# Reading streamed weights straight from their inputs instead of from a contiguous scratch copy, with separate tail buffers, in a recurrent-memory kernel

## The chip, the cores and the metric

The kernel runs on one core of one Trainium2 chip. The metric is the device time of one execution in microseconds (us), taken as the median of several executions.

The views name the engines thus: PE is TensorE (matmuls) and PEld its weight loads, DVE is VectorE, ACT is ScalarE, POOL is GpSimd; SP is SyncE, which here only issues loads and stores (DMA transfers). HBM is the memory that holds the inputs and the scratch. The granted clock is the share of TensorE's full clock that the profile shows.

## The reference

Two layer pairs A, B, A, B over a sequence of 2048 tokens of width 640. A is attention in 64 segments of 32 tokens with 8 memory rows; segment s needs the memory that segment s-1 left, so A is a recurrence. B is a token-mixing MLP. All tensors are bf16.

```python
def _A_ref(x, mem0, Wq, Wk, Wv, Wo, seg_len):     # 32 heads of 192, M = 8 memory rows
    for s in range(n_seg):                          # 64 segments of 32 tokens, one after the other
        h = jnp.concatenate([mem, xs], axis=1)      # 40 rows
        q, k, v = ...                               # h @ Wq, Wk, Wv: each 640 x 6144
        o = softmax(mask(q k^T * scale)) v          # per head
        o = jnp.einsum('bhte,hed->btd', o, Wo)      # 6144 x 640
        mem = o[:, :M, :]; outs.append(o[:, M:, :])
def _B_ref(x, w1, w2, w3, w4):
    h = gelu(layernorm(x) @ w1)                     # 640 x 640
    ...                                             # shift a quarter of the columns by -1, +1, -2, +2 tokens
    x1 = x + shifted @ w2                           # 640 x 640
    return x1 + gelu(layernorm(x1) @ w3) @ w4       # 640 x 1536 x 640
x = x + A(LN(x)); x = x + B(LN(x)); x = x + A(LN(x)); x = x + B(LN(x))
```

## The kernel before

The kernel runs both A layers as two lanes, the second lane 6 segments behind the first, so there are 70 recurrent steps of 80 rows. In each step the attention weights are used once. They are cut into 64 half-weights of 480 KB ([128, 1920] bf16): q, k, v and output weights, 8 head groups, 2 halves. 37 of them stay resident, 27 are streamed in every step through a ring of 6 buffers. The weights of B (13 pieces w1 to w4, some 6.7 pieces per step on average) go through the same ring. Loads are issued in program order on SP's queue.

At the start the kernel copies the 27 streamed half-weights (on ACT's queue) and all of B's weights (on POOL's queue) from the inputs into scratch in HBM, laid out so that each of the 128 partitions reads one contiguous piece of 3840 B:

```python
RING_BUFS = 6
N_RES_HALVES = 37 if B2X else 26
RELAYOUT = 1
...
def w_src(kind, g, hf):
    if kind == "q":
        return Wq_v[:, :, GW * g + GWH * hf:GW * g + GWH * (hf + 1)]     # [128, 5, 384]: runs of 768 B
    ...
    return Wo_v[:, g, GCH * hf:GCH * (hf + 1), :]                        # [128, 3, 640]: runs of 1280 B
...
if RELAYOUT == 1:
    for u_ in streamed:                                                  # 27 half-weights
        nc.scalar.dma_start(out=w_view(wS[stream_idx[u_]], kind), in_=w_src(kind, g, hf))
        relaid.add(u_)
...
zt = wringB.tile([P, HSZ], bf16, name=BNAME)
nc.vector.memset(zt[:], 0.0)
for i, (nm, a, b, used) in enumerate(BP):                                # B's weights into scratch wB
    if nm == "w1":
        nc.gpsimd.dma_start(out=dst, in_=w1_v[:, :, a * P:b * P])
    ...                                                                  # w3, w4 alike
    else:                                                                # w2: zero, then the used rows
        nc.gpsimd.dma_start(out=wB[i][:, 0:used], in_=zt[:, 0:used])
        ...

def get_wB(nm, a):
    t = wringB.tile([P, HSZ], bf16, name=BNAME)                          # the shared ring
    nc.sync.dma_start(out=t[:, 0:used], in_=wB[i][:, 0:used])
    return bp_view(t, nm, a_, b_)

def get_w(kind, g, hf):
    if u_ in resident:
        return resident[u_]
    if u_ in res_set:                                                    # first use, in step 0
        nc.sync.dma_start(out=w_view(t, kind), in_=w_src(kind, g, hf))
        ...
    t = wring.tile([P, HSZ], bf16, name="wst")
    if RELAYOUT and u_ in relaid:
        nc.sync.dma_start(out=t[:], in_=wS[stream_idx[u_]])              # contiguous
    else:
        nc.sync.dma_start(out=w_view(t, kind), in_=w_src(kind, g, hf))   # original layout
```

After step 69 a tail is left: the last blocks of B. They share single buffers (`xw`, `bu`, `vT`, `bv_c`), and gelu has one scratch tile `g_sq`, so a chunk of gelu must be over before the next one begins:

```python
def gelu2(z_ps, out_ap, shape):
    sq = work.tile([P, GELU_W], f32, name="g_sq", bufs=1)
    nc.scalar.activation(out=sqv, in_=z_ps, func=ACT.Square)
    nc.vector.tensor_scalar(...); nc.vector.tensor_tensor(...)
    nc.scalar.activation(out=thv, in_=sqv, func=ACT.Tanh, scale=GELU_C)
    nc.vector.scalar_tensor_tensor(out=out_ap, ...)
...
def sA():                                          # b2x_stages: first of a block's stages
    xw = work.tile([XB, Dm], f32, name="xw", bufs=1)
    ...                                            # load rows of x1d, x3d
    u = work.tile([XB, Dm], f32, name="bu", bufs=1)
```

## Time and profile before

| | |
|---|---|
| median | 4443.05 us (4 runs), 4448.39 us (16 runs, with those beside the changed kernel) |
| step 1 begins (start) | 143.1 us |
| step 1 to step 69, start to start (middle) | 4153 us, 61.1 us a step from step 4 on |
| last attention matmul to the end (tail) | 85.4 us |

Each step opens with one matmul that clears the accumulator `psy`, so its start times cut the run into steps. This is the view of that source line between 130 and 230 us; the last columns are the first and the last start in the window:

```profile
L515 PE MATMUL psy<-zer x2: 337/337/337, 143.1 to 195.2; 128*128 128x400 bf16 x2
```

The table of stretches of the kernel before has, after each stretch, the busy us of PE, PEld (weight loads), DVE, ACT and POOL with the number of instructions, then the granted clock, the DMA share and GB/s:

```profile
0.00:50.00 50.00, 11.04 (x143) 9.11 (x143) 10.12 (x30) 0.00 (x0) 22.30 (x48) 0.90 0.99 355
50.00:100.00 50.00, 9.72 (x122) 7.89 (x123) 4.37 (x13) 8.32 (x27) 1.58 (x6) 0.56 1.05 365
100.00:150.00 50.00, 41.10 (x777) 35.22 (x774) 18.82 (x51) 18.91 (x74) 3.55 (x12) 0.97 1.06 366
200.00:4200.00 4000.00, 3579.76 (x67338) 3191.89 (x67402) 2465.50 (x6597) 1846.26 (x6917) 517.09 (x1423) 0.96 0.82 277
```

The first three rows are the start: DMA share at or above 0.99, 355 to 366 GB/s, and PE busy for only 21 of the first 100 us. (The share is the sum of packet times over 16 engines; the records of the first 100 us show up to 23 packets in flight at once, so it can pass 1.) The last row is the middle: DMA share 0.82, PE busy 3580 of 4000 us. What PE waits for there (engine, line, waited for, us in all, times, longest us):

```profile
PE pso L654 <- ACT PT L372: 155.7, 128, 10.8
PE psy L675 <- DVE oT L374: 114.5, 129, 1.7
PE pss L610 <- DVE kT L374: 100.1, 32, 7.9
...
PE y2A L1069 <- DMA wst<-wB: 1.8, 4, 0.8
...
PEld L675 <- DMA wst<-wS: 0.7, 1, 0.7
```

PE's large waits are for PT on ACT and for oT and kT on DVE, the handoffs of attention. For weights (`wst` is a buffer of the ring) it waits 1.8 us in 4000 at this line and 2.3 us in all; its weight loads (PEld) wait 0.9 us. DMA is busy for four fifths of the time, and PE is hardly ever held up by it.

In the tail, PE's last transposes for attention begin at 4358.36 us, and the two remaining blocks end with ACT's copy of `bv_c`. Timeline of the kernel before (start us, us, engine, line, what; in brackets the idle time before it and what ended it):

```profile
4358.36 0.47 PE L696 MATMUL psyt<-ident,yT 128*80 128x128 bf16 x5 [0.58 <-ACT yT L685]
...
4405.49 0.72 ACT L1083 CAST bv_c<-xw 128x640 bf16<-128x640 f32 x1 [3.63 <-DVE xw L1073]
...
4406.94 0.62 ACTq L962 DMA_DIRECT2D xw<-x3d  x1
...
4421.32 0.61 DVE L409 TENSOR_SCALAR bv_c<-bu,lnmv_b,lnrs_b 128x640 bf16<-128x640 f32 x1 [0.73 <-POOL lnrs_b L404]
...
4425.27 0.49 ACT L419 ACTIVATE g_sq<-psh 128x384 f32<-128x384 f32 x1 [1.85 <-PE psh L1056]
...
4428.05 0.49 ACT L419 ACTIVATE g_sq<-psh 128x384 f32<-128x384 f32 x1 [0.68 <-DVE h2T L423]
...
4438.98 0.72 ACT L1083 CAST bv_c<-xw 128x640 bf16<-128x640 f32 x1 [3.28 <-DVE xw L1073]
```

The first block ends with the copy at 4405.49. Only then is the second block's `xw` loaded (4406.94), and its layer norms run until 4421.3 (the last `bv_c<-bu` on DVE). The Square steps of gelu (`ACT ACTIVATE g_sq<-psh`) then follow each other at 2.8 us (4425.27, 4428.05), one chunk at a time.

### The profile page before, as it was taken

What the parts mean: (1) busy time and instruction counts of PE and PEld (TensorE: products, weight loads), DVE (VectorE), ACT (ScalarE), POOL (GpSimd) and SP (SyncE); (2) the same over time, 40 slices, a digit from 0 to 9 for tenths busy, and PEclk for the clock granted to TensorE, in tenths of its full rate; (3) what the DMA queues carried; (4) which work ended last, traced back from release to release, by engine and by line L of the source; (5) the groups of instructions that cost most, each with busy time, mean ns of one, the idle gap of its engine ahead of it and who ended that gap; (6) DMA issues with size and microseconds to landing.
All of it is one profiled execution on the core that took longest, in us unless ns stands there. A gap on an engine that the chain in (4) does not pass through costs nothing. (4 is left out here: it accounts for less than half of the span.)

```text
span 4443.2 us, 168838 instructions
## 1 busy us (share of the span) xinstructions
PE 3867.6 (87%) x72349; PEld 3440.2 (77%) x72420; DVE 2650.9 (60%) x7089; ACT 1988.7 (45%) x7427; POOL 577.5 (13%) x1578
## 2 busy tenths in 40 slices
PE   2798989898889988898988999988998988989895
PEld 2687878787778887787877888877887877888883
DVE  1455656666656666666666666666666666566654
ACT  1444444444444444444444444444444444444442
POOL 2111111111111111111111111111111111111110
PEclk7999999999999999999999999999999999999997
DMA  9887878888888788888888888888888888888884
GB/s 358 295 271 255 275 270 272 282 284 276 279 288 279 266 283 278 281 285 277 277 275 277 294 283 280 269 275 281 288 277 289 275 273 286 282 278 275 272 276 162
DMA packets 404193, 1232.59 MB, mean 277 GB/s; under 512 B 47080, under 2 KB 88176, under 8 KB 403440
## 3 DMA queue, kind: packets, MB, share of 16 engines
q1 hardware_dynamic: 378632, 1190.97, 78.9%
q10 hardware_dynamic: 21016, 23.76, 1.7%
q8 instruction: 566, 9.27, 0.8%
q0 software_dynamic: 3792, 7.05, 0.4%
q14 instruction: 187, 1.53, 0.1%
HBM read 1202.10 MB, written 38.50 MB: 279 GB/s over the span
## 5 line engine op out<-in xcount | busy, mean ns | idle before, releaser
L624 ACT ACTIVATE Pm<-pss,nb 80x80 bf16<-80x80 f32 x2240 | 699.5, 320 | 292.2 <-DVE nb L619 210.3
L568 PEld LDWEIGHTS <-hT 128*80 128x80 bf16 x5600 | 617.5, 119 | 211.4 <-issue 2.2
L372 ACT CAST V<-psv 80x384 bf16<-80x384 f32 x1120 | 507.4, 479 | 361.7 <-PE psv L568 277.5
L568 PE MATMUL psv<-wv,hT 128*80 128x384 bf16 x3500 | 663.9, 327 | 1.2 <-DMA wv<-in_A_Wv_dram 1.2
L374 DVE CAST oT<-pso 128x480 bf16<-128x480 f32 x560 | 367.5, 656 | 478.4 <-PE pso L659 476.2
L530 PEld LDWEIGHTS <-wst 128*128 128x128 bf16 x14700 | 637.2, 104 | 3.8 <-DMA wst<-wS 2.7
L374 DVE CAST kT<-psk 128x480 bf16<-128x480 f32 x560 | 364.7, 651 | 424.3 <-PE psk L530 422.6
L592 POOL COPY Vz<-V 80x128 bf16<-80x128 bf16 x560 | 169.1, 302 | 2887.0 <-ACT V L372 2874.3
L530 PE MATMUL psq<-hT,wq 128*128 128x80 bf16 x10500 | 497.4, 207 | 29.9 <-ACT hT L494 17.9
L530 PEld LDWEIGHTS <-wq 128*128 128x128 bf16 x10500 | 455.4, 103 | 38.5 <-issue 29.4
L372 ACT CAST qT<-psq 128x480 bf16<-128x480 f32 x560 | 307.6, 549 | 383.0 <-PE psq L530 381.1
L675 PE MATMUL psy<-oT,wst 128*128 128x80 bf16 x7350 | 361.0, 204 | 123.2 <-DVE oT L374 121.0
L675 PE MATMUL psy<-oT,wo 128*128 128x80 bf16 x9450 | 445.8, 204 | 1.5 <-DMA wo<-in_A_Wo_dram 1.5
L624 ACT ACTIVATION_READ_ACCUMULATOR Pm<-pss,nb 80x1 f32 x2240 | 442.1, 197 | 0.0
L675 PEld LDWEIGHTS <-wst 128*128 128x128 bf16 x7350 | 318.2, 101 | 151.9 <-issue 146.9
L568 PE MATMUL psv<-wst,hT 128*80 128x384 bf16 x2100 | 418.8, 331 | 1.2 <-DMA wst<-wS 1.1
L530 PE MATMUL psk<-hT,wst 128*128 128x80 bf16 x8400 | 411.7, 206 | 1.4 <-DMA wst<-wS 1.3
L530 PE MATMUL psk<-hT,wk 128*128 128x80 bf16 x8400 | 410.2, 206 | 2.9 <-DMA wk<-in_A_Wk_dram 2.9
L675 PEld LDWEIGHTS <-wo 128*128 128x128 bf16 x9450 | 388.4, 102 | 1.9 <-DMA wo<-in_A_Wo_dram 1.9
L372 ACT COPY PT<-pst 80x320 bf16<-80x320 bf16 x560 | 242.4, 433 | 274.0 <-PE pst L642 226.5
L610 PEld LDWEIGHTS <-qT 128*80 128x80 bf16 x3360 | 228.0, 123 | 168.1 <-issue 114.0
L374 DVE CAST kTz<-psk 64x160 bf16<-64x160 f32 x1120 | 351.9, 314 | 10.3
(122 smaller groups left out, 5896.5 us busy)
## 6 DMA issues: line engine op xcount, KB each, us to landing
wst<-wS SPq DMA_DIRECT2D x1890, 480.0 KB, 4.9
wst<-wB SPq DMA_DIRECT2D x395, 480.0 KB, 5.2
wst<-wB SPq DMA_DIRECT2D x71, 320.0 KB, 4.7
x1d<-xs SPq DMA_DIRECT2D x64, 80.0 KB, 4.0
xs<-x2d SPq DMA_DIRECT2D x64, 80.0 KB, 3.5
x3d<-xs SPq DMA_DIRECT2D x64, 80.0 KB, 3.5
xw<-x1d ACTq DMA_DIRECT2D x31, 160.0 KB, 3.9
x2d<-xw SPq DMA_DIRECT2D x31, 160.0 KB, 5.4
```

The costliest lines, as they stand in the source:

```text
L372: nc.scalar.copy(out=out_ap, in_=in_ap)
L374: nc.vector.tensor_copy(out=out_ap, in_=in_ap)
L530: nc.tensor.matmul(out=psq[:, c, :], lhsT=w[:, kc, cc * P:(cc + 1) * P], rhs=hT[:, kc, :], start=(kc == 0), stop=(kc == KC - 1))
L568: nc.tensor.matmul(out=psv[:], lhsT=hT[:, kc, :], rhs=wv[:, kc, :], start=(kc == 0), stop=(kc == KC - 1))
L592: nc.gpsimd.tensor_copy(out=vz[:, :, 0, 0:64], in_=V3[:, SS, 0:64])
L610: nc.tensor.matmul(out=o_, lhsT=l_, rhs=r_, start=False, stop=(n == len(ops) - 1))
L624: nc.scalar.activation(out=E[:, i, :], in_=pss[:, i, :], func=ACT.Exp, bias=nb[:], scale=scale, accum_out=sums[:, i:i + 1])
L675: nc.tensor.matmul(out=cx.psy[:, m, :], lhsT=wo[:, cc, m * P:(m + 1) * P], rhs=oT[:, c, :], start=False, stop=last)
```

## The change

The intent is to leave out the copies at the start and to read the weights from the inputs in every step; the price is shorter packets. Only w2 keeps its scratch copy, because its pieces are padded with zeros. In the tail, the blocks get alternate buffers, under tags whose attention tiles are no longer in use, and gelu gets three scratch tiles. Flags of other variants (`B_MERGE`, `RELAY_SPREAD`) are added but off. The core of the diff, with cuts:

```diff
-RELAYOUT = 1
+WB_LATE = 1
+B_MERGE = 0
+TAIL_ALT_TAGS = 1
+RELAY_SPREAD = 0
+RELAYOUT = 0
...
-        zt = wringB.tile([P, HSZ], bf16, name=BNAME)
-        nc.vector.memset(zt[:], 0.0)
-        for i, (nm, a, b, used) in enumerate(BP):
-            ... (all of w1, w2, w3, w4 into wB)
+        def setup_wB():
+            zt = h2T[:].rearrange("p f x -> p (f x)")
+            for i, (nm, a, b, used) in enumerate(BP):
+                if nm != "w2":
+                    continue
+                ... (zero rows, then w2's rows, on POOL's queue)
...
         def get_wB(nm, a):
             t = wringB.tile([P, HSZ], bf16, name=BNAME)
-            nc.sync.dma_start(out=t[:, 0:used], in_=wB[i][:, 0:used])
-            return bp_view(t, nm, a_, b_)
+            v = bp_view(t, nm, a_, b_)
+            if nm == "w1":
+                nc.sync.dma_start(out=v, in_=w1_v[:, :, a_ * P:b_ * P])
+            elif nm == "w3":
+                nc.sync.dma_start(out=v, in_=w3_v[:, :, a_ * P:b_ * P])
+            elif nm == "w4":
+                nc.sync.dma_start(out=v, in_=w4_v[:, a_:b_, :])
+            else:
+                nc.sync.dma_start(out=t[:, 0:used], in_=wB[i][:, 0:used])
+            return v
...
-    def gelu2(z_ps, out_ap, shape):
+    def gelu2(z_ps, out_ap, shape, tag=None):
+        if tag is None:
+            sq = work.tile([P, GELU_W], f32, name="g_sq", bufs=1)
+        else:
+            sq = work.tile([P, GELU_W], f32, name="g_sq_alt", tag=tag, bufs=(3 if PIPE_DEEP else 2))
...
+        alt = bool(TAIL_ALT_TAGS) and t >= T_A and t == T_A + (T_A % 2)
+        tg_x = "xs1" if alt else None
+        alt_g = bool(TAIL_ALT_TAGS) and t >= T_A
+        tg_v = "V" if alt_g else "vT"
...
-            xw = work.tile([XB, Dm], f32, name="xw", bufs=1)
+            xw = work.tile([XB, Dm], f32, name="xw", bufs=1) if not alt else work.tile([XB, Dm], f32, name="xw_alt", tag=tg_x)
... (bu, vT, v2T and bv_c alike; gelu2(..., tag=(tg_v if alt_g else None)))
...
+        if B2X and t >= 1 and wB_pending:
+            wB_pending.pop()()
```

More of the change, by code (lines that the diff above doesn't have):

```diff
@@ L283, with emit_relayout @@
     relaid = set()
-    if RELAYOUT == 1:
-        for u_ in streamed:
+    relay_pending = list(streamed) if RELAYOUT == 1 else []
+    def emit_relayout(n):
+        for _ in range(min(n, len(relay_pending))):
+            u_ = relay_pending.pop(0)
             kind, g, hf = u_
@@ L288 @@
             relaid.add(u_)
+    if RELAYOUT == 1 and not RELAY_SPREAD:
+        emit_relayout(len(relay_pending))
     def chunks3(n):
@@ L312, in bp_view @@
             return ap2d[:, 0:(b - a) * Dm].rearrange("p (v d) -> p v d", v=b - a)
-        zt = wringB.tile([P, HSZ], bf16, name=BNAME)
-        nc.vector.memset(zt[:], 0.0)
-        for i, (nm, a, b, used) in enumerate(BP):
-            dst = bp_view(wB[i], nm, a, b)
-            if nm == "w1":
-                nc.gpsimd.dma_start(out=dst, in_=w1_v[:, :, a * P:b * P])
-            elif nm == "w3":
-                nc.gpsimd.dma_start(out=dst, in_=w3_v[:, :, a * P:b * P])
-            elif nm == "w4":
-                nc.gpsimd.dma_start(out=dst, in_=w4_v[:, a:b, :])
-            else:
-                nc.gpsimd.dma_start(out=wB[i][:, 0:used], in_=zt[:, 0:used])
-                for v_ in range(a, b):
-                    kc, p0, p1, off = W2P[v_]
-                    nc.gpsimd.dma_start(out=dst[p0:p1, v_ - a, :], in_=B_w2[kc * P + p0:kc * P + p1, :])
+        def setup_wB():
+            zt = h2T[:].rearrange("p f x -> p (f x)")
+            for i, (nm, a, b, used) in enumerate(BP):
+                dst = bp_view(wB[i], nm, a, b)
+                if nm != "w2":
+                    continue
+                else:
+                    for z0 in range(0, used, Dm):
+                        nc.gpsimd.dma_start(out=wB[i][:, z0:z0 + Dm], in_=zt[:, 0:Dm])
+                    for v_ in range(a, b):
+                        kc, p0, p1, off = W2P[v_]
+                        nc.gpsimd.dma_start(out=dst[p0:p1, v_ - a, :], in_=B_w2[kc * P + p0:kc * P + p1, :])
+        wB_pending = [setup_wB]
+        if not WB_LATE:
+            wB_pending.pop()()
         def get_wB(nm, a):
@@ L412 @@
     GELU_W = max(6 * XS, 3 * XB) if B2X else 6 * XS
-    def gelu2(z_ps, out_ap, shape):
+    def gelu2(z_ps, out_ap, shape, tag=None):
         _, a_, b_ = shape
-        sq = work.tile([P, GELU_W], f32, name="g_sq", bufs=1)
+        if tag is None:
+            sq = work.tile([P, GELU_W], f32, name="g_sq", bufs=1)
+        else:
+            sq = work.tile([P, GELU_W], f32, name="g_sq_alt", tag=tag, bufs=(3 if PIPE_DEEP else 2))
         sqv = sq[:, 0:a_ * b_].rearrange("p (a b) -> p a b", a=a_)
@@ L946, in b2x_stages @@
         TOK = 2 * SEG
+        alt = bool(TAIL_ALT_TAGS) and t >= T_A and t == T_A + (T_A % 2)
+        tg_x = "xs1" if alt else None
+        alt_g = bool(TAIL_ALT_TAGS) and t >= T_A
+        tg_v = "V" if alt_g else "vT"
+        if alt:
+            bvt = work.tile([XB, Dm], bf16, name="bv_alt", tag="xs0")
+        else:
+            bvt = bv_c
         def sA():
-            xw = work.tile([XB, Dm], f32, name="xw", bufs=1)
+            xw = work.tile([XB, Dm], f32, name="xw", bufs=1) if not alt else work.tile([XB, Dm], f32, name="xw_alt", tag=tg_x)
             if any((not v) or kp == NP2 or kp == 0 for (_, _, _, kp, v) in items):
@@ L965, in sA @@
                     nc.gpsimd.dma_start(out=xl_c[Lb:4:2, :], in_=src[TOK * kp + TOK - 2:TOK * kp + TOK, :])
-            u = work.tile([XB, Dm], f32, name="bu", bufs=1)
+            u = work.tile([XB, Dm], f32, name="bu", bufs=1) if not alt else work.tile([XB, Dm], f32, name="bu_alt", tag=tg_x)
             st.u, st.xw, st.ranges = u, xw, ranges
@@ L972, in sA @@
             layer_norm(xw, u, slice(0, XB))
-            layer_norm(u, bv_c, slice(0, XB))
+            layer_norm(u, bvt, slice(0, XB))
             layer_norm(xl_c, xl_c, slice(0, 4))
@@ L983, in sA3 @@
         def sA3():
-            ln_apply(st.h2, bv_c)
+            ln_apply(st.h2, bvt)
             ln_apply(st.hl2, xl_c)
@@ L989, in sB @@
             for kc in range(KC):
-                nc.tensor.transpose(out=psvT[:, kc, :], in_=bv_c[:, kc * P:(kc + 1) * P], identity=ident[:, :])
+                nc.tensor.transpose(out=psvT[:, kc, :], in_=bvt[:, kc * P:(kc + 1) * P], identity=ident[:, :])
             psl = ps_tile([P, KC, XP], bf16, "psl")
@@ L993, in sB @@
                 nc.tensor.transpose(out=psl[:, kc, :], in_=xl_c[0:XP, kc * P:(kc + 1) * P], identity=ident[0:XP, 0:XP])
-            vT = work.tile([P, KC, XB + 4], bf16, name="vT", bufs=1)
+            vT = work.tile([P, KC, XB + 4], bf16, name="vT", bufs=1) if not alt else work.tile([P, KC, XB + 4], bf16, name="vT_alt", tag=tg_v, bufs=(3 if PIPE_DEEP else 2))
             evac(vT[:, :, 0:XB], psvT[:], "act")
@@ L1009, in f @@
                     nc.vector.tensor_copy(out=hTB[:, :, 0:4, :], in_=hTB[:, :, TOK:TOK + 4, :])
-                gelu2(psh[:, 0:b - a, :], hTB[:, a:b, 4:4 + TOK, :].rearrange("p k w l -> p k (w l)"), [P, b - a, XB])
+                gelu2(psh[:, 0:b - a, :], hTB[:, a:b, 4:4 + TOK, :].rearrange("p k w l -> p k (w l)"), [P, b - a, XB], tag=(tg_v if alt_g else None))
                 if last:
@@ L1035, in sD @@
             else:
-                layer_norm(u, bv_c, slice(0, XB))
+                layer_norm(u, bvt, slice(0, XB))
         def sD2():
-            ln_apply(st.h3, bv_c)
+            ln_apply(st.h3, bvt)
         def sE():
@@ L1043, in sE @@
             for kc in range(KC):
-                nc.tensor.transpose(out=psv2T[:, kc, :], in_=bv_c[:, kc * P:(kc + 1) * P], identity=ident[:, :])
-            v2T = work.tile([P, KC, XB + 4], bf16, name="v2T", tag="vT", bufs=1)
+                nc.tensor.transpose(out=psv2T[:, kc, :], in_=bvt[:, kc * P:(kc + 1) * P], identity=ident[:, :])
+            v2T = work.tile([P, KC, XB + 4], bf16, name="v2T", tag="vT", bufs=1) if not alt else work.tile([P, KC, XB + 4], bf16, name="v2T_alt", tag=tg_v, bufs=(3 if PIPE_DEEP else 2))
             evac(v2T[:, :, 0:XB], psv2T[:], "act")
@@ L1057, in f @@
                                          rhs=v2T[:, kc, 0:XB], start=(kc == 0), stop=(kc == KC - 1))
-                gelu2(psh2[:, 0:b - a, :], h2T[:, a:b, :], [P, b - a, XB])
+                gelu2(psh2[:, 0:b - a, :], h2T[:, a:b, :], [P, b - a, XB], tag=(tg_v if alt_g else None))
             return f
@@ L1082, in sG @@
                 else:
-                    nc.scalar.copy(out=bv_c[:], in_=xw[:])
-                    nc.sync.dma_start(out=dst[t0_ + j0:t0_ + j1, :], in_=bv_c[2 * j0 + Lb:2 * j1:2, :])
+                    nc.scalar.copy(out=bvt[:], in_=xw[:])
+                    nc.sync.dma_start(out=dst[t0_ + j0:t0_ + j1, :], in_=bvt[2 * j0 + Lb:2 * j1:2, :])
         has_new = any(v and kp < NP2 for (_, _, _, kp, v) in items)
@@ L1103, in b2x_stages, with mg @@
         stages.append(sG)
+        if B_MERGE and LN_SPLIT and has_new and t < T_A:
+            def mg(f1, f2):
+                return lambda: (f1(), f2())
+            i3 = stages.index(sA3)
+            stages[i3:i3 + 2] = [mg(sA3, sB)]
+            i5 = stages.index(sD2)
+            stages[i5:i5 + 2] = [mg(sD2, sE)]
+            if len(stages) > NG:
+                rest = stages[NG:]
+                spread = []
+                for f in rest:
+                    spread += [f, None]
+                stages = stages[:NG] + spread
         return stages
@@ L1112 @@
     for t in range(TT):
+        if RELAY_SPREAD and t >= 1 and relay_pending:
+            emit_relayout(RELAY_SPREAD)
+        if B2X and t >= 1 and wB_pending:
+            wB_pending.pop()()
         if B2X:
```

## The prediction

> **What bounds it now.** There are 70 recurrent steps and a tail. From 200 to 4350 us the stretch table has PE busy about 0.90, DVE 0.62, ACT 0.46, DMA 0.82. A step takes 61 us. The waits of PE there name ACT PT (158 us), DVE oT (118) and DVE kT (102); waits for DMA sum to about 3 us. So the middle is bound by PE and its handoffs, not by DMA. The ends differ. Start: step 1 begins only at 143 us; until then DMA share is 0.99 to 1.06 (about 52 MB), PE busy 11 of the first 50 us and 10 of the next 50. Tail: the last step ends near 4367 us, then two blocks of the second layer run one after the other, to 4406 and to 4443 us (chain that ended last).
>
> **What the change does.**
> 1. It drops the copies of 27 streamed half-weights and of the second layer's weights (except w2) into contiguous scratch. Step 0 still loads 64 half-weights of 480 KB once. Packet records: 768 B takes 36 ns, 1280 B 55 ns, 3840 B 149 ns clean (179 on average in the middle). 48 halves x 40 packets x 36 ns plus 16 x 24 x 55 ns per DMA engine are about 90 us, so I estimate step 1 to begin near 100 us: gain 43 us (35 to 50).
> 2. In every step the streamed loads read the original layout: five 768 B (q, k, v) or three 1280 B (output weights) packets per partition in place of one of 3840 B. Clean cost per load and engine: 1.19 us becomes 1.44 or 1.32. The Trainium skill, "DMA: Bandwidth & Descriptors", Specifications, puts line rate at 512 B and above; this trace differs: 768 B moves 21.3 B/ns, 3840 B 25.8. This adds some 470 us of 16-engine time: DMA share 0.82 to about 0.9, packets 0.40 to about 1.37 million. The order of loads and of PE's work stays beyond the first steps. Loads now land 4.9 us after issue (median), then wait 4.5 us (median; lowest 5%: 0.9) for first use. Landing 0.3 to 1 us later, few become late, mainly w4 chunks and q/k ones: loss 20 us (estimate), up to 90.
> 3. The tail gets alternate buffers: the second block's load and three layer norms (4407 to 4422 us) move under the first block, and gelu chunks (2.8 us each in series) overlap down to DVE's 1.5 us. Gain 24 us (15 to 30).
>
> **Sum.** 4443 - 43 - 24 + 20 = about 4396 us, 1.1% faster. Range (8 in 10) 4355 to 4445. Faster by over 2%: 0.08; within 2%: 0.84; slower by over 2%: 0.08.
>
> **What would show it.** Step 1 beginning at 95 to 108 us; middle DMA share near 0.9 with steps still 61 to 61.5 us; PE's waits for wst growing from 3 us to tens of us; issue to landing rising to 5.3 to 6.5 us; after the last step, 76 us shrinking to about 52.
>
> **What would make it wrong.** The large risk is the middle: the queue is near saturation, and lateness grows steeply. If the stray slow packets (179 against 149 ns) grow with the number of packets, each load costs 1.7 to 1.9 us against 1.75 us of PE time per load, and steps become DMA-bound: 100 to 300 us lost. If they come from the scratch copy, or vanish when the queue is backed up (768 B packets averaged 37 ns in the start), the loss is nil, and the result near 4375.

## More of the kernel before

Executions of one and the same kernel spread by about 1% here (4420.64 to 4464.68 us for the kernel before, 16 runs), so effects below some 10 us are read from the trace, not from the total.

## The result, and the profile after

The changed kernel takes 4392.28 us (median of 10 runs, 4381.82 to 4399.65), against 4448.39 us (16 runs). Its time over that of the kernel before is 0.9875 (95% interval 0.9856 to 0.9893). All ratios here are the mean time of one kernel's fast runs over that of the other's of the same rounds, so not quite the ratio of the medians. The outputs are correct.

In the profiled runs (4443.2 and 4384.4 us) the 58.8 us come from these parts:

| part | before | after | difference |
|---|---|---|---|
| start: to the beginning of step 1 | 143.1 us | 101.9 us | -41 |
| middle: step 1 to step 69 | 4153 us | 4158 us | +4 |
| step 69 itself | 61.5 us | 61.6 us | 0 |
| tail: last attention matmul to the end | 85.4 us | 63.4 us | -22 |

The opening matmul of steps 1 and 2 after (L537 is the old L515):

```profile
L537 PE MATMUL psy<-zer x2: 337/338/338, 101.9 to 153.9; 128*128 128x400 bf16 x2
```

The stretches of the changed kernel:

```profile
0.00:50.00 50.00, 32.08 (x373) 24.89 (x373) 17.44 (x50) 11.76 (x39) 19.07 (x51) 0.80 1.02 322
50.00:100.00 50.00, 35.63 (x528) 28.10 (x524) 13.80 (x37) 14.43 (x57) 2.93 (x10) 0.83 1.09 338
100.00:150.00 50.00, 46.99 (x934) 41.77 (x935) 25.25 (x69) 23.86 (x90) 5.92 (x19) 1.00 1.01 307
200.00:4200.00 4000.00, 3582.40 (x67454) 3194.04 (x67518) 2464.28 (x6584) 1848.59 (x6927) 512.27 (x1417) 0.96 0.92 278
```

PE now works from the first slice on (32 of the first 50 us, where it was 11). The start is still bound by DMA: share 1.02 and 1.09. In the middle the DMA share rose from 0.82 to 0.92 at the same 277 to 278 GB/s: the same bytes take more engine time. PE's busy time there is 3582 us where it was 3580. The queue lines of the two pages (queue, packets, MB, share of 16 engines), before and then after:

```profile
q1 hardware_dynamic: 378632, 1190.97, 78.9%
q10 hardware_dynamic: 21016, 23.76, 1.7%
```

```profile
q1 hardware_dynamic: 1367304, 1190.97, 89.1%
...
q10 hardware_dynamic: 5096, 10.49, 0.8%
```

1.37 million packets in place of 0.38 million move the same 1190.97 MB. PE's waits in the middle, after:

```profile
PE pso L676 <- ACT PT L391: 167.2, 124, 6.8
PE psy L697 <- DVE oT L393: 115.6, 130, 1.7
PE pss L632 <- DVE kT L393: 87.0, 31, 6.0
...
PEld L552 <- DMA wst<-in_A_Wk_dram: 2.3, 5, 0.9
...
PE psk L552 <- DMA wst<-in_A_Wk_dram: 1.5, 4, 0.8
```

PE's waits for weights are 1.5 us in 4000 (2.3 before), those of its weight loads 2.5 us (0.9 before). Next to nothing of the longer loads reached PE. The tail, after:

```profile
4321.67 0.47 PE L718 MATMUL psyt<-ident,yT 128*80 128x128 bf16 x5 [0.58 <-ACT yT L707]
...
4350.78 0.61 DVE L428 TENSOR_SCALAR bu<-xw,lnmv_b,lnrs_b 128x640 f32<-128x640 f32 x1 [0.27 <-POOL lnrs_b L423]
...
4354.29 0.61 DVE L428 TENSOR_SCALAR bv_c<-bu,lnmv_b,lnrs_b 128x640 bf16<-128x640 f32 x1 [0.26 <-POOL lnrs_b L423]
...
4363.33 0.72 ACT L1113 CAST bv_alt<-xw_alt 128x640 bf16<-128x640 f32 x1 [3.28 <-DVE xw_alt L1103]
...
4371.62 0.49 ACT L441 ACTIVATE g_sq_alt<-psh 128x384 f32<-128x384 f32 x1 [1.91 <-PE psh L1086]
4373.22 0.49 ACT L441 ACTIVATE g_sq_alt<-psh 128x384 f32<-128x384 f32 x1 [1.11 <-PE psh L1086]
...
4380.93 0.72 ACT L1113 CAST bv_c<-xw 128x640 bf16<-128x640 f32 x1 [2.67 <-DVE xw L1103]
```

The second block's layer norms (`bu<-xw` at 4350.78, `bv_c<-bu` at 4354.29) now lie before the first block's end (4363.33), and the Square steps follow each other at 1.6 us. From the transposes at 4321.67 the first block takes 42.4 us (47.9 before); from its end to the end of the program, with the second block, it is 20.3 us more (37.0 before).

### The profile page after: what moved, and what is told of

The parts are those of the page before. It is cut to its first block, busy times and chain, and to the rows that moved or that the text cites. A ratio compares the mean times of both kernels' runs of the same rounds, so it can differ in the third digit from the quotient of the medians.

```text
span 4384.4 us, 168796 instructions
## 1 busy us (share of the span) xinstructions
PE 3877.9 (88%) x72349; PEld 3446.1 (79%) x72420; DVE 2649.8 (60%) x7088; ACT 1988.7 (45%) x7427; POOL 571.7 (13%) x1573
## 3 DMA queue, kind: packets, MB, share of 16 engines
q1 hardware_dynamic: 1367304, 1190.97, 89.1%
## 5 line engine op out<-in xcount | busy, mean ns | idle before, releaser
L552 PEld LDWEIGHTS <-wk 128*128 128x128 bf16 x8400 | 351.4, 102 | 5.7 <-DMA wk<-in_A_Wk_dram 5.7
```

The costliest lines, as they stand in the source:

```text
L552: nc.tensor.matmul(out=psq[:, c, :], lhsT=w[:, kc, cc * P:(cc + 1) * P], rhs=hT[:, kc, :], start=(kc == 0), stop=(kc == KC - 1))
```

## The experiments

Theory: the total is a sum of three separate parts. The start shrinks because it is bound by DMA time and there is less of it. The middle does not move, because the loads have slack before PE needs them and a step's DMA time stays under 61 us. The tail shrinks through its buffers. Rivals: the second layer's (B's) copies alone hold the start; the tail gains from the direct loads; the layout does cost the middle, and noise hides it; the middle is free because slow packets vanish when the queue is backed up.

"Step" below is the mean step from step 4 to step 69 of the profiled run. Over all runs of the two layouts with 37 resident half-weights and 6 buffers it varies from 60.9 to 61.5 us without order, so a difference of 0.3 us in it (20 us in all) means nothing in a single profile.

### Which part of the change gives which part of the gain

**tail_only**: the kernel before, with the tail's alternate buffers alone (the changed kernel with `RELAYOUT = 1` and the old copying and loading of B's weights).

> The kernel before with the tail's alternate buffers alone. Additive theory (start -41, middle about +4, tail -22 us): 22 us less than before, ratio 0.995; step 1 still begins at 143 us, 63 us from the last attention matmul to the end in place of 85. Rival (the tail gained because the last weight loads come straight from the inputs, not from the buffers): no gain, tail stays at 80 to 85 us, ratio 0.999 to 1.000.

Measured: ratio 0.9954 (0.9927 to 0.9981), median 4434.55 us against 4454.58. Step 1 begins at 145.1 us and the tail is 66.3 us. So the buffers shorten the tail without any direct load; the rival falls.

**tail_off**: the changed kernel with

```diff
-TAIL_ALT_TAGS = 1
+TAIL_ALT_TAGS = 0
```

> The changed kernel without the tail's alternate buffers. Additive theory: 37 us less than before, ratio 0.9917; step 1 begins at 102 us, tail 85 us, steps 61.2 us. Rival (direct loading speeds the tail, not the buffers): tail near 63 us, ratio 0.987.

Measured: ratio 0.9907 (0.9881 to 0.9934), 4413.8 us. Step 1 begins at 100.8 us, the tail is 85.6 us, a step 61.27 us. The direct loads do nothing for the tail. The two halves of the change add up: 0.46% and 0.93% make 1.39%, where the whole gave 1.25% (0.0107 to 0.0144).

**a_direct**: the kernel before with

```diff
-RELAYOUT = 1
+RELAYOUT = 0
```

> The kernel before with only the attention weights loaded straight from the inputs; the second layer's weights are still copied to scratch at the start and read from there, and the tail is as before. If the start is bound by DMA time alone: 27 copies of 1.44 us less, 27 loads 0.24 us slower, so about 32 us off, step 1 at 110 to 116 us; ratio 0.993. Rival (it is the second layer's copies, which go first in the queue of POOL, that hold the start): step 1 at 130 us or later, ratio 0.997 or more. In the middle DMA share 0.90.

Measured: ratio 0.9917 (0.9891 to 0.9943), 4418.79 us. Step 1 begins at 114.9 us, a step is 60.9 us, the DMA share from 200 to 4300 us is 0.90.

**b_direct**: the changed kernel with

```diff
-TAIL_ALT_TAGS = 1
+TAIL_ALT_TAGS = 0
-RELAYOUT = 0
+RELAYOUT = 1
```

> The changed kernel with the attention weights still copied to scratch at the start, without the tail's buffers; only the second layer's weights come straight from the inputs, w2 copied late. If the start is bound by DMA time alone: some 6 MB of copies less, 15 to 18 us off, step 1 at 125 to 129 us, ratio 0.996. Rival (the second layer's copies hold the start): step 1 at 115 us or earlier, ratio 0.994 or less. In the middle DMA share 0.83.

Measured: ratio 0.9976 (0.9947 to 1.0005), 4439.06 us. Step 1 begins at 130.3 us, a step is 61.31 us, the DMA share 0.83.

The opening matmul of step 1, a_direct first, then b_direct:

```profile
L515 PE MATMUL psy<-zer x1: 337/337/337, 114.9 to 114.9; 128*128 128x400 bf16 x1
```

```profile
L537 PE MATMUL psy<-zer x1: 337/337/337, 130.3 to 130.3; 128*128 128x400 bf16 x1
```

So dropping the attention copies takes 28 us off the start and dropping B's copies 13 us; together they make the 41 us of the changed kernel. The start is a sum of DMA work, and no single queue holds it. Both estimates from DMA time (32 and 15 to 18 us) were a little too high.

### Is the middle really free, and why

**spread**: the changed kernel, with the attention copies brought back, two per step from step 1 on, so that from step 15 on the layout would be contiguous again:

```diff
-RELAY_SPREAD = 0
-RELAYOUT = 0
+RELAY_SPREAD = 2
+RELAYOUT = 1
```

> The changed kernel, but the contiguous scratch for the attention weights comes back bit by bit: two half-weights are copied to it per step from step 1 on, and each is read from it once it is copied (from step 15 on all are); step 0 reads straight from the inputs, so the start stays at 102 us. DMA share in the middle back near 0.83. My theory (the direct layout costs the middle little, 0 to 16 us): total within 15 us of the changed kernel, ratio to before 0.983 to 0.990. Rival (the middle does lose the 20 to 40 us that more DMA time could cost, hidden in the noise): 20 to 40 us faster than the changed kernel, ratio 0.979 to 0.983.

Measured: ratio 0.9932 (0.9908 to 0.9955), 4423.28 us, so neither number came true. Step 1 began at 132.8 us, not at 102. The timeline of ACT shows why:

```profile
0.81 0.73 ACTq L294 DMA_DIRECT2D wS<-in_A_Wq_dram  x1
...
47.13 0.64 ACTq L294 DMA_DIRECT2D wS<-in_A_Wq_dram  x1
...
61.23 0.56 ACTq L294 DMA_DIRECT2D wS<-in_A_Wk_dram  x1
```

The copies depend on nothing, and all 27 were issued in step 0, from 0.81 to 85.5 us; their place in the program's loop meant nothing. Which source a load reads is fixed by the program, though: loads of attention weights still come straight from the inputs until 922 us, fewer in each step. But the run still answers the question about the middle, because from step 14 on, small shifts of the order aside, it is the changed kernel with contiguous loads of the attention weights. Stretch from 300 to 4200 us, spread first, then the changed kernel:

```profile
300.00:4200.00 3900.00, 3498.93 (x65831) 3116.11 (x65829) 2407.65 (x6438) 1798.23 (x6753) 498.02 (x1385) 0.96 0.84 278
```

```profile
300.00:4200.00 3900.00, 3494.52 (x65785) 3116.12 (x65849) 2408.96 (x6438) 1804.55 (x6763) 500.20 (x1383) 0.96 0.91 278
```

DMA share 0.84 against 0.91, PE busy 3499 against 3495 us, steps 61.16 against 61.21 us, step 1 to 69 in 4155 against 4158 us. From step 15 to step 69, where all attention loads of spread are contiguous, a step takes 61.00 against 61.01 us. The direct layout costs the middle nothing that can be seen; the total of spread is 31 us above the changed kernel's, and its start 31 us longer.

**res31_after, res34_after**: the changed kernel with fewer resident half-weights, so 33 or 30 streamed per step in place of 27:

```diff
-N_RES_HALVES = 37 if B2X else 26
+N_RES_HALVES = 31 if B2X else 26      (res34_after: 34)
```

> The changed kernel with 31 resident half-weights in place of 37, so 33 streamed per step in place of 27. Theory (the middle is free only while the DMA time of a step stays under the step's 61 us; 768 B packets cost 41.6 ns in the middle, busy or not, so 1.66 us per load): 33 x 1.61 + 6.5 x 1.6 + 2 = about 65 us of DMA time per step, so the middle becomes DMA-bound: steps of 64 to 67 us, DMA share 1.0 or more, PE waits for wst over 100 us in all, total about 4640 us, ratio 1.045. Rival (slow packets vanish when the queue is backed up, 1.44 us per load): 57 us of DMA time, steps stay under 62 us, ratio under 1.00.

> The changed kernel with 34 resident half-weights, 30 streamed per step, between the 27 of the changed kernel (steps 61.2 us, DMA share 0.92) and the 33 of the run before (64.9 us, share 1.00). Theory: 30 x 1.61 + 12 = 60 us of DMA time per step against 61 us of the other work: at the edge, steps 61.8 to 63 us, share 0.97 or 0.98, PE waits for wst 20 to 80 us in all, total 4430 to 4510 us, ratio 0.995 to 1.015. If the loss grows in proportion to packets instead (half of the 3.7 us per step), steps are 63 us or more.

**res31_before**: the same edit (31) in the kernel before.

> The kernel before with the same 31 resident half-weights: same extra loads from the contiguous scratch, 1.44 us each with the slow packets. Theory: 39.5 x 1.44 + 2 = 59 us of DMA time per step, just under the 61 us: steps 61 to 62.5 us, DMA share about 0.95, start some 7 us longer (more copies), ratio 1.003 to 1.02. If the layout of the loads does not matter, it is as slow per step as the changed kernel with 31.

Measured:

| kernel | streamed per step | ratio to before | step | DMA share, 300 to 4200 us |
|---|---|---|---|---|
| changed | 27 | 0.9875 | 61.2 us | 0.91 |
| res34_after | 30 | 0.998 (0.9949 to 1.001) | 62.2 us | 0.97 |
| res31_after | 33 | 1.0433 (1.0398 to 1.0468) | 64.9 us | 1.00 |
| before | 27 | 1 | 61.1 us | 0.82 |
| res31_before | 33 | 1.0046 (1.0005 to 1.0086) | 61.6 us | 0.91 |

The stretch lines of res31_after and then res31_before:

```profile
300.00:4200.00 3900.00, 3401.45 (x61838) 2952.90 (x61895) 2278.29 (x6072) 1704.16 (x6353) 456.35 (x1293) 0.95 1.00 307
```

```profile
300.00:4200.00 3900.00, 3480.05 (x65392) 3087.29 (x65452) 2399.23 (x6399) 1784.22 (x6714) 483.80 (x1375) 0.97 0.91 324
```

And PE's largest waits for weights in the same window of res31_after:

```profile
PE y2A L1099 <- DMA wst<-in_B_w_dram: 40.6, 116, 1.8
PE psk L552 <- DMA wst<-in_A_Wk_dram: 19.0, 49, 0.8
...
PE psh L1086 <- DMA wst<-in_B_w_dram: 11.0, 32, 0.6
PE psv L590 <- DMA wst<-in_A_Wv_dram: 8.7, 21, 1.0
```

With 33 loads a step, the direct layout fills DMA's time, and the step becomes what the DMA time says: 65 us expected, 64.9 measured. (A share of 1.00 alone would not prove this, since the start showed up to 1.09; the match of step and DMA time is the stronger sign.) With 30 loads it is at the edge, as expected: share 0.97, PE's waits for wst 35 us. Read contiguously, the same extra loads cost 0.5 us a step; there the share was expected as 0.95 and came out at 0.91, for the 3840 B packets took 169.6 ns on average and not 179.5. The expected waits of res31_after (over 100 us) are met within the precision of the view: PE's waits for wst sum to 99 us, those of PEld, which may overlap with them, to 135 us. Engine time, not bytes, is what runs out: res31_before moves 324 GB/s at a share of 0.91, res31_after only 307 GB/s at 1.00. The rival falls: 768 B packets took 41.6 ns on average in the middle of the changed kernel, 41.2 ns in res31_after; they do not get back to the clean 36 ns (the median in the changed kernel) when the queue is full. (These means are over the packet records between 1000 and 4300 us.)

**ring4_after, ring4_before**: both kernels with fewer stream buffers.

```diff
-RING_BUFS = 6
+RING_BUFS = 4
```

> The changed kernel with 4 stream buffers in place of 6. Theory (the later landing of the direct loads is absorbed by the slack that 6 buffers give): a replay of the load and use times of the kernel before with 4 buffers puts 91 to 125 us of waits into the middle, steps 62.5 to 63 us, PE waits for wst near 100 us, total about 4490 us, ratio 1.01. Rival (the slack plays no part): steps still 61.2 us, ratio 0.9875.

> The kernel before with 4 stream buffers in place of 6. Theory: the replay puts 24 to 50 us of waits into the middle, steps 61.4 to 61.9 us, total about 4480 us, ratio 1.008; so with 4 buffers the direct layout costs 60 to 75 us more in the middle than the contiguous one, where with 6 it costs none that is seen. Rival: no difference between the two layouts in the middle.

Measured: ring4_after 1.0431 (1.0393 to 1.0469), 4641.13 us, steps 64.8 us, DMA share 0.88; ring4_before 1.0422 (1.038 to 1.0463), 4639.82 us, steps 64.0 us, DMA share 0.80. PE's waits for weights from 300 to 4200 us, ring4_before:

```profile
PE y2A L1069 <- DMA wst<-wB: 39.0, 66, 2.9
PE psy L675 <- DMA wst<-wS: 34.2, 48, 2.2
PE psq L530 <- DMA wst<-wS: 32.1, 37, 2.4
...
PE psk L530 <- DMA wst<-wS: 10.5, 17, 1.9
```

The totals with 4 buffers are equal, although the changed kernel starts 42 us earlier and its tail is 19 us shorter; so its middle is some 60 us longer (53 us between the starts of steps 1 and 69 in the profiles). The difference of the layouts came out near the low end of what was expected (60 to 75 us) or just under it, and this with free DMA time: it is lateness, not capacity. Pairing each load's issue, landing and first use (as at the end of this text) shows the slack: from issue to first use it is 6.1 us (before) and 6.2 us (changed) with 4 buffers, where it is 9.3 us in both kernels with 6, and between landing and first use only 1.2 and 0.8 us are left, where it was 4.5 and 3.9 us. The size of the loss itself was expected wrong: 24 to 50 us for the kernel before where nearly 190 us were lost (2.9 us a step over 65 steps), 91 to 125 us for the changed kernel where the middle grew by 244 us. The replay only knew buffers and DMA time. It kept the old order on SP's queue, where weight loads stand in line with the stores and loads of rows, and with 4 buffers the built kernel has another order there (219 of the 2716 issues on that queue stand elsewhere). Whether that is the cause was not tested.

### The parts of the tail, and the rest of the start

**tail_blocks**: the changed kernel with gelu's single scratch tile, the blocks' buffers kept:

```diff
-gelu2(psh[:, 0:b - a, :], ..., tag=(tg_v if alt_g else None))
+gelu2(psh[:, 0:b - a, :], ..., tag=None)                          (both calls)
```

> The changed kernel, with the gelu scratch of the tail single again; the two blocks keep their separate buffers. Predicted parts of the tail's gain: 16 us from the second block's load and layer norms moved under the first, 8 us from overlapped gelu chunks. So the tail should be 63 + 8 = 69 to 71 us and the total 8 us above the changed kernel, ratio 0.989. Rival (most of the gain is the gelu overlap): tail 75 us or more.

Measured: ratio 0.9878 (0.9858 to 0.9898), 4399.6 us; tail 72.2 us. So 9 us of the tail's gain come from gelu's scratch tiles and 13 us from the blocks' buffers; the total is too noisy to tell the 9 us, the trace tells it.

**w2_after0**: the changed kernel issues its copies of w2 not in step 1 but at 6.7 to 30 us, since they too depend on nothing. Here the zero rows are made from the output of step 0:

```diff
-            zt = h2T[:].rearrange("p f x -> p (f x)")
+            yf = pending_xnew[0].yT[:].rearrange("p k n -> p (k n)")
+            zt = const.tile([P, Dm], bf16, name="zw")
+            for z0 in range(0, Dm, KC * NS):
+                z1 = min(Dm, z0 + KC * NS)
+                nc.vector.tensor_scalar_mul(out=zt[:, z0:z1], in0=yf[:, 0:z1 - z0], scalar1=0.0)
```

> The changed kernel, with the zero rows for w2's scratch computed as 0 times the output of step 0, so that the 2.1 MB of w2 copies cannot start before step 0 ends (in the changed kernel they are issued from 7 us on, though the code means them for step 1). If the start is bound by DMA time: 2.1 MB at 330 GB/s are 6 us, so step 1 begins at 95 to 98 us in place of 102, and the rest stays: total 4 to 6 us below the changed kernel, ratio 0.986 to 0.987. Rival (step 0 is held by the chain of loads and matmuls, not by DMA time): step 1 still at 101 to 102 us. The first second-layer block may wait for w2 if it comes too late: then the stretch from step 1 to step 4 grows beyond 182 us.

Measured: ratio 0.9869 (0.9849 to 0.989), 4400.11 us against 4451.99. Step 1 begins at 96.5 us, as DMA time says. But step 1 then takes 60.7 us where it took 51.9, and from step 1 to step 4 it is 188.5 us (178.7 in the changed kernel), beyond the 182 us that the expectation warned of. PE's waits in step 1 of w2_after0:

```profile
PE psk L556 <- DMA wst<-in_A_Wk_dram: 2.2, 2, 2.0
...
PE psv L594 <- DMA wst<-in_A_Wv_dram: 1.4, 1, 1.4
```

The changed kernel has 0.4 us of such waits in its step 1. The copies, now in step 1, stand beside its streamed loads, and loads come late; PE's waits for wst in step 1 are 4.2 us in all, 3.8 us more than in the changed kernel, of the 8.7 us. The granted clock from 100 to 150 us was also lower (0.93 against 1.00); how much of the rest that explains was not tested. What the start saved is given back either way. The interval overlaps that of the changed kernel, and no kernel is shown to be faster than it.

## Why the prediction was right

- The total was predicted as 4396 us, 1.1% faster, and came out at 4392.28 us, ratio 0.9875. That the two are only 4 us apart is in part luck: the prediction took 47 us off a median of 4 runs (4443.05 us), and measured against the 16 runs (4448.39 us) the change is 56 us. The chance put on "within 2%" (0.84) was on the right side.
- Start: predicted -43 us with step 1 near 100 us, measured -41 us and 101.9 us. The mechanism is shown by a_direct and b_direct (28 + 13 us), and once more by w2_after0.
- Tail: predicted -24 us, measured -22 us, shown by tail_only and tail_off. The parts, which the prediction did not size, were put at 16 and 8 us before tail_blocks ran and measured as 13 and 9 us.
- Middle: the DMA share rose to 0.92 (predicted 0.9), packets to 1.376 million (1.37), landing after issue to 5.3 to 5.6 us (5.3 to 6.5), steps stayed at 61.2 us. The added engine time was somewhat less than predicted: the main queue's packets took 400 us more of 16 engines' time, not 470. The term that was mis-sized most is "loss 20 us (estimate), up to 90": in the profiles it is 4 us, inside the noise, and spread shows the same step with contiguous loads. The step of the argument that failed is "few become late": hardly any did. PE's waits for wst did not grow "to tens of us", but went from 2.3 to 1.5 us on PE and from 0.9 to 2.5 us on its weight loads. Pairing issues, landings and first uses between 200 and 4300 us (for the loads whose landing was recorded, 842 of 2241 before and 560 of 2246 after) shows where the delay went: median landing 4.9 us after issue before and 5.4 after; median wait for first use 4.5 us and then 3.9; issue to first use 9.3 us in both, for these loads and for all. The loads' later landing was taken out of their waiting time.
- The risk that the prediction named, stray slow packets that grow with their number, did not come. A 3840 B packet took 179.5 ns on average in the middle before, 30 ns over its clean time. Five 768 B packets took 208 ns after, 28 ns over theirs, and three of 1280 B 186 ns, 21 ns over theirs. So the excess of a load did not grow with its number of packets; what causes it was not tested. The steep edge that it warned of is there, but further on, between 30 and 33 loads a step.
- The Trainium skill, "DMA: Bandwidth & Descriptors", Specifications, gives 512 B as the smallest transfer for line rate. The changed kernel's weight packets (768 and 1280 B) lie above it, and yet the same 1190.97 MB on the main queue took 89.1% of 16 engines' time in place of 78.9%. The measurement decides.

## What to carry to other kernels

A layout copy pays only if a limit that it relieves is the binding one: here the contiguous copy saved DMA time in a stage where each load had 4.5 us to spare, and its price stood at the start, where DMA was the limit. Before trading packet size against copies, add up the DMA time per step (packets times measured time per packet) and compare it with the step, and look at the wait between landing and first use; here the trade was free until either ran out, and then it cost at once (steps of 61.2, 62.2, 64.9 us for 27, 30, 33 loads, and of 64.8 us with 4 buffers). A DMA that depends on nothing may be issued much earlier than its place in the loop says, as the copies of spread were, so read its issue time in the trace before believing that work was put off.

## What the Trainium skill lacked or had wrong

- "DMA: Bandwidth & Descriptors", Specifications, puts line rate at 512 B and above; this point is about that row alone. In these traces the median packet takes 36 ns for 768 B and 55 ns for 1280 B (changed kernel) and 149 ns for 3840 B (kernel before), so 21.3, 23.3 and 25.8 B/ns: five packets of 768 B cost 21% more engine time than one of 3840 B.
- No page read for this case gives how long a packet of a given size takes in a loaded queue. In the middle the means were 179.5 ns for 3840 B (kernel before), 41.6 ns for 768 B and 62.1 ns for 1280 B (changed kernel): 31, 28 and 21 ns over the median for 3840 B in one, five or three packets.
